# One fused attention and feed-forward kernel on one core: its hand-listed order of steps replaced by another list, with the products of no use gathered in one place

## The chip, the cores and the metric

The kernel runs on one core of a Trainium2 chip. The metric is the time of one execution on the device, in microseconds. A core has a matrix engine (TensorE, "PE" in the profile, with its weight loads as "PEld"), a vector engine (VectorE, DVE), a scalar engine with function tables (ScalarE, ACT), a general engine (GpSimd, POOL) and an engine that here does nothing but issue transfers (SyncE, SP). Each engine takes its own instructions strictly in their listed order and waits, where it must, on the others.

## The reference

```python
# x: (8, 8, 512, 64)   state: (8, 8, 32, 64)   w_in: (512, 2048)   w_out: (2048, 512)
scale = 1 / np.sqrt(64)
a  = softmax(scale * x @ state.T)        # per block and head: 512 x 32
xread = a @ state                        # 512 x 64
a2 = softmax(scale * state @ x.T)        # 32 x 512
sread = a2 @ x                           # 32 x 64
y = concat([xread, sread], rows)         # 8 blocks of 544 tokens, 512 wide (8 heads x 64)
h = y @ w_in                             # 4352 x 2048
g = h * erf(log(1 + exp(h)))
out = g @ w_out                          # 4352 x 512, f32
```

The two weights come in 8-byte floating point, and the kernel turns them into f32 on chip.

## The kernel before

*Stages.* The eight blocks b have 512 tokens each that come from `xread`; the 32 `sread` tokens of all eight blocks are put together into one small unit, the states. The hidden width of 2048 is done in two halves. In half A all blocks go through attention and through the first 1024 hidden columns, with weights held in `w_in` and `wo[0]`; the output rows are stored from SP. Then the second half of both weights is brought back from DRAM (`wi`, `wo`), and half B goes through the same blocks with kept `y` from DRAM; its outputs are added to the stored rows by transfers from POOL, those of the last block by DVE. Most products are computed in two-by-two quarters with seven products in place of eight (names ending in 1 to 7), which needs sums of quarters on DVE (y.1 to y.4, M1 to M4, A1 to A4, T1 to T4).

*Steps and their list.* Every piece of work is a named step, put into a table by `step(name, f, ...)`. The string `ORDER` (from L18) lists all steps by hand; a loop at the kernel's end issues them in that order, and `in_order` ties each instruction to the one before it on its engine, so that the list is the order on PE, DVE, ACT, SP and POOL alike. Nothing else schedules. Waits between engines follow from the tiles that the steps share; a step placed early in the list of an engine makes all behind it on that engine wait for its data.

A word of the form `~k*n` is no step: it is n products of a 128x128 matrix by itself into bank k of PSUM, whose result nothing reads (`warm`, L367). The step `warm` at the very start is eight such products.

*The steps that matter here.* Names with a block number b = 1 to 7 come once for each block.

- The start, block 0. `lx0` to `lx3` load x of block 0 (L282: even ones are issued from ACT, odd ones from SP), `lst0` to `lst8` the states (L287, L306). `x0` to `x3` transpose x on PE (four products each), `x0c` to `x3c` copy the results out of PSUM, `s0` turns block 0's states. `q0`, `q1` are the scores, copied out by `q00c` to `q11c`; `tm0`, `tm1` transpose them; `max`, `less`, `exp`, `sum`, `inv`, `norm` are the softmax of group 0 and 1 on DVE and ACT; `ta0`, `ta1` transpose the weights back.
- The weights. `piece(kind, j)` makes the steps of 256 columns of `w_in` (kind i) or rows of `w_out` (kind o): `i0l0`, `i0l1` load its two halves (L338, 512 KB each, SP), `i0a0` (L342) and `i0a1` (L345) are conversions on ACT, `i0v0`, `i0v1` (L347, L349) on DVE; piece i0 alone is converted in two parts (`i0+a0` ...). `a0` uses another function table of ACT than the softplus and than the error function. Pieces 4 to 7 are kept in DRAM for half B (`i4k` ...).
- Block 0's first unit. `n00`, `n01`, `n02`, `n10`, `n12` multiply the states by `w_in` (L852), `u0`, `u1` transpose the states of the other blocks (L950; they need all of `lst1` to `lst8`), `h0` to `h7` are the hidden columns (L863) with softplus `h0s` ... (through L611) and copies `h0c` ..., `h0e` ... (L878) the error functions of two at a time, `h0g` ... the products with h, `o00` to `o36` the second products (L884), stored by `o0c`, `o0d` ....
- The second attention of block 0: `big`, `wt`, `wz`, `wn` the softmax, `tw0`, `tw1` (transposes on PE) with copies `tw0c`, `tw1c` on ACT into `a2T`, `rd0` (L464) the product of a2 and x, `rn0`, `rt0`, `rc0` what follows it.
- The attention of block b: `a{b}xq0` to `7` load x transposed (L295, SP), `a{b}tx` turn it on DVE, `a{b}s` the scores (L490), the softmax on DVE and ACT down to `a{b}ta`; then the second attention: `a{b}ey` (ACT), `a{b}ty` (DVE, turns), **`a{b}kz` stores the turned weights to DRAM (L529, SP), `a{b}z0` to `z3` load them back in another layout (L300, SP)**, `a{b}x0` to `x3` load x (L290, SP), and **`rd{b}` (L464) multiplies the two on PE**, followed by `rn`, `rt`, `rc`.
- The hidden part of block b: `A{b}m` (L573) multiplies states and `w_in`, `A{b}f01` to `f17` are the products (L622, in `hidden`), with copies (L230) on ACT and softplus (L611) `..s11` to `..s22`, then `e0`, `e1` (error function, L630) and `g0`, `g1` (DVE). `A{b}p10` to `p71` are the second products (L672, in `one_level`), `A{b}d0` to `d3` the stores (L652). `SA`, `SB` are the states' unit in half A and B, `B{b}...` those of half B, whose second products go two levels deep (L738, in `inner`).

*Buffers.* Block b and b+1 share most tiles: `at`, `cv`, the two slots of `ring`, eight PSUM banks. So a step of one block often waits until a step of the block before has read its tile.

Line numbers here and in the profile are those of the kernel before; in the changed kernel every line behind the list has a number one lower.

Of the kernel before, what the change touches and what calls it, by code (L numbers as in the profile page):

```python
# [46 lines left out]
i7a1 a3kz A3f05 y33 a4xq0 A3M4 A3f11 A3f0u2 a3x2 A3f07 a4tx1 A2p11 A3f0s11 y34 A2A1 A3f0u3 i7a0
A3f0c22 A3f04 a3z2 A1pc21 A1pc12 A3f03 a3z1 A3f0c21 i7v0 a3z3 A2p50 A3f1c a4tx3 a3z0 A2pc a3iy
a4xq5 A3f0c12 a4tx0 A3f12 yk2 A2A3 A1d0 A3f16 A3f1c11 yk3 i7v1 A3f0s21 rd3 A1d1 A3f1u2 A3f0s12
A3f17 rn30 A3f0s22 rn31 A2A2 rt3 A3f15 A3f1u3 rc3 a4tx2 A3f14 A3f1c22 a4s A2A4 A3e0 A3f13 a5xq3  # L50
A2p60 A3f1c21 A3f1c12 o4l1 a4c0 A1d3 a4c1 a4tu0 a5xq2 A2p61 a4mx0 a4tu1 yl3 A3f1s11 A1d2 a4my0
A3f1s21 A4m i7k a4mx1 A2pu2 o4l0 A3f1s22 a4my1 a5xq6 A3f1s12 a4sb1 A2p70 a4sb0 a5xq4 a4ex0 a4x3
A2p71 a4ex1 a4sm0 a5xq1 A4m00 a4sm1 A4m01 a4x1 A2p51 A4m10 a4iz o5l1 a4nm0 A2pu3 a5xq5 A4m11 a4ta0
A2p20 a4nm1 a4ms A4M1 A3e1 a4ta1 A4f01 y41 A4M3 A2p40 A4M2 y42 y44 a4ey1 A2p21 a5tx1 A4f0c A3g1
a4ey0 A4f02 A4f06 A4f0c11 A2pc22 A4f05 A4f0u2 a4ty1 A2pc11 y43 A4f11 A4M4 o4a0 A4f07 a4ty0 A3g0
A2p41 a4kz A4f0u3 a5xq7 a4x2 A2p30 A2pc21 A3A3 o4a1 A3A1 A2p31 a4z3 A3p10 A4f0c22 a4z0 a4z1 o4v0
a4x0 a5tx2 A3p11 a5xq0 a5tx3 A3A2 a4z2 A4f04 A2d0 A3pc o4v1 A4f03 A4f0c21 a4iy A3p60 A4f1c A2pc12
o4k yl4 A4f0c12 A2d1 A4f16 A4f0s12 rd4 A4f1u2 A4f0s22 A4f17 A4f0s11 rn41 a5x3 rn40 a5tx0 A4f0s21
A2d3 rt4 A4f15 A3A4 rc4 o5l0 A4f1u3 a5s A4f1c22 A4f14 a5c1 a6xq6 a5c0 A4f13 A4f1c21 a6xq0 a5tu0
A4f12 a5my0 a5x2 A3p20 a5mx0 A4e0 a6xq5 a5tu1 a5sb0 a5x0 A3p61 a5mx1 a6xq4 a5sb1 o6l0 A4f1c12  # L60
A3p50 a5ex0 a6xq3 a5my1 a5ex1 o5a0 a5sm1 a6xq2 A5m a5sm0 a6xq7 a5iz a5ms a5nm0 a5ey0 A3p51 a5nm1
A4f1c11 a5ta0 A5m00 A3pu2 o5v0 A5m11 A5f01 a5ta1 A5m10 y51 A3p70 a5ey1 A5M1 A5m01 y53 y52 A5f0c
a5ty0 A3p71 A5M2 a5ty1 A4f1s22 A5f06 a5iy A5M3 o5a1 a5kz a6xq1 a6tx1 A5f02 A3pu3 A5f05 A5f0u2 o6l1
A3pc22 A5f0c11 a6tx2 A5f07 o5v1 A5f11 A5f0u3 A4f1s21 A3p30 y54 a6tx3 A4f1s11 a5z0 A4f1s12 A4g0
a5x1 a5z2 A5f04 a5z3 A3p31 A4e1 a5z1 a6tx0 A3d3 o5k A5M4 A3p40 yl5 A5f0c22 A2d2 A4g1 A5f0c21 yk4
A5f1c A5f03 o6a1 A5f16 A5f0c12 rd5 A5f1u2 A5f17 rn51 rn50 A4A1 rt5 A5f15 rc5 A5f1u3 a6s A5f1c22
A5f12 A5f0s11 a7xq3 a6c1 A5f14 a6c0 a7xq5 a6tu1 A5f13 A5f1c21 a6my0 A5f0s21 a7xq0 A3p21 A5f1c12
a6tu0 a7xq2 a6mx0 A3p41 A3pc11 a6x1 A4A2 A5f1c11 a7xq4 a6sb0 A4p10 a7xq6 a6mx1 a6ex0 a6my1 A3pc21
a7xq1 A4p11 a6sb1 a6sm0 o7l1 a6ex1 a7xq7 o6a0 a6sm1 A6m a6iz a6x0 A4pc a6nm0 yk5 a6nm1 A4p20 A6m00
a6ms a6ta0 A6m10 A3pc12 A6m11 y61 a6ey0 A6f01 A3d1 a6ta1 a6x3 A6m01 A6M1 A4p60 a6x2 A6f0c a6ty0  # L70
# [6 lines left out]
A7m01 A7m10 a7iz a7nm0 A4p41 a7my0 A4pc11 A7m00 a7ta0 A7m11 A7f01 A7M1 a7nm1 A5p10 A7f0c a7ms y71
a7ey0 a7ta1 a7ey1 A7M2 A7f05 y72 A4pc21 y73 A7f02 A5A3 A4d2 A7f06 A4d1 A6f0s11 a7x1 y74 A5p11 A5A1
o7a1 A4d0 a7x3 a7ty1 A6f1s22 A5p50 A6f0s21 A5A2 A5pc o7a0 a7ty0 A5p60 A7M3 a7kz A6f1s12 A5A4 A5p61
o7v0 o7v1 A5p51 A5pu2 A6f0s12 A6f1s11 A5p70 A7f0u2 A7f0c11 a7z0 A6f0s22 a7z1 A5p71 a7x0 a7z2 a7z3  # L80
A7f07 o7k A5pu3 A6f1s21 A7f11 A5pc22 A7f0u3 a7iy A5d3 A5p30 A7f0s11 yl7 A5p31 A6e1 A7f04 A7f0c22
A7M4 rd7 A7f0c21 A7f1c A7f03 rn71 wo rn70 rt7 A7f16 A7f0c12 A7f12 A7f1u2 A7f15 A7f1c11 rc7 A7f17
# [973 lines left out]
```

## Time and profile before

| | us |
|---|---|
| three runs | 709.36, 711.31, 711.01 |
| their median | 711.01 |
| the profiled execution | 710.65 |
| span of its instructions | 708.9 |
| mean granted clock of PE in it | 0.998 |

The span is what the views below cut up; the profiled execution's own time is 1.75 us longer. The page's slices show where PE is not full: each digit is a fortieth of the span, 17.7 us, in tenths.

```
PE   8879999999999999999999999999999999999997
DVE  4759899978788969566433649698969597889482
ACT  2999998899588866855135675678675675775720
DMA  8867687859677832741051232214333313151535
```

The groups of instructions that PE spends most of its time in, with count, busy time and mean time of one:

| line and step | products | busy us | mean ns |
|---|---|---|---|
| L672, second products of half A | 840 + 168 | 189.8 + 37.7 | 380 |
| L622, hidden products | 480 + 360 | 121.4 + 90.9 | 382, 380 |
| L738, second products of half B (the largest of its groups) | 588 | 73.0 | 275 |

ACT loads a function table 71 times in all, 1.28 us each; of these 31 stand at the softplus (L611), with 39.8 us.

Start of one product to start of the next takes 0.43 us for 128x256, 0.22 for 128x128 at full clock, as the timeline shows them one behind the other.

### The profile page before, as it was taken

How to read it: one execution, taken by the hardware profiler on the slowest of the kernel's cores; microseconds unless marked ns; L12 is line 12 of the kernel's file. 1: busy time of each engine (PE TensorE's matmuls, PEld its weight loads, DVE VectorE, ACT ScalarE, POOL GpSimd, SP SyncE). 2: the span in 40 equal slices, each digit the busy share in tenths (PEclk: the TensorE clock that was granted, in tenths of full speed). 3: DMA queues.
4: the chain of work that ended last, by engine and by line, in shares of the span. 5: the costliest groups of instructions: out<-in, count | busy, mean ns of one | idle time of the engine just before them, and what ended most of it. 6: DMA issues, size and time to landing. Idle time of an engine off the chain costs nothing.

```text
span 708.9 us, 12281 instructions
## 1 busy us (share of the span) xinstructions
PE 695.3 (98%) x4931; PEld 582.1 (82%) x4931; DVE 524.4 (74%) x717; ACT 481.0 (68%) x709; POOL 37.7 (5%) x38
## 2 busy tenths in 40 slices
PE   8879999999999999999999999999999999999997
...
DVE  4759899978788969566433649698969597889482
ACT  2999998899588866855135675678675675775720
...
DMA  8867687859677832741051232214333313151535
GB/s 263 202 190 133 194 200 209 193 179 244 186 172 224 207 130 87 216 147 48 16 193 45 90 111 26 58 21 93 40 73 36 78 19 65 16 97 31 83 75 105
DMA packets 136441, 84.96 MB, mean 120 GB/s; under 512 B 93760, under 2 KB 127552, under 8 KB 136128
## 3 DMA queue, kind: packets, MB, share of 16 engines
...
q10 hardware_dynamic: 544, 0.52, 0.2%
...
## 4 chain that ended last, share of the span: by engine, by line
PE 91%; ACT 4%; DMA 1%; issue 0%; DVE 0%; SPq 0%; DVEq 0%; ACTq 0%
PE b L672 31%; PE b L622 26%; PE b L738 22%; PE b L573 4%; PE b L924 4%; PE b L884 2%; PE b L464 1%; PE b L490 1%; DMA at<-in_x_dram 1%; ACT ring L611 1%; ACT L611 1%; ACT ring L345 0%; ACT L342 0%; ACT ring L230 0%; PE b L863 0%
## 5 line engine op out<-in xcount | busy, mean ns | idle before, releaser
L672 PE MATMUL b<-ta,ring 128*128 128x256 f32 x840 | 189.8, 380 | 0.0
L672 PEld LDWEIGHTS b<-ta,ring 128*128 128x128 f32 x840 | 158.3, 190 | 26.6 <-issue 3.4
L230 ACT COPY ring<-b 128x512 f32<-128x512 f32 (+1 forms) x138 | 79.6, 584 | 86.4 <-PE b L622 63.3
L622 PE MATMUL b<-y,m 128*128 128x256 f32 x480 | 121.4, 382 | 1.4 <-ACT ring L230 1.2
L622 PEld LDWEIGHTS b<-y,m 128*128 128x128 f32 x480 | 88.0, 190 | 17.3 <-issue 3.5
L230 ACT COPY res<-b 128x512 f32<-128x512 f32 (+2 forms) x98 | 52.1, 537 | 71.1 <-PE b L672 35.2
L222 DVE TENSOR_TENSOR ring<-ring,b 128x512 f32<-128x512 f32 (+1 forms) x71 | 46.7, 661 | 67.9 <-PE b L622 25.1
L622 PE MATMUL b<-sy,m 128*128 128x256 f32 x360 | 90.9, 380 | 0.0
L224 DVE TENSOR_TENSOR ring<-ring 128x2048 f32<-128x2048 f32 (+1 forms) x36 | 77.8, 2164 | 9.1 <-ACT ring L630 8.8
L611 ACT ACTIVATE ring<-ring 128x512 f32<-128x512 f32 x128 | 76.4, 629 | 5.3 <-DVE ring L222 5.0
L622 PEld LDWEIGHTS b<-sy,m 128*128 128x128 f32 x360 | 65.7, 190 | 10.2 <-issue 1.3
L223 DVE TENSOR_TENSOR ring<-ring 128x1024 f32<-128x1024 f32 (+2 forms) x65 | 73.2, 1137 | 0.3
L738 PE MATMUL b<-at,ring 128*128 128x128 f32 x588 | 73.0, 275 | 0.0
L738 PEld LDWEIGHTS b<-at,ring 128*128 128x128 f32 x588 | 71.4, 192 | 1.6
L650 POOL DMA_DIRECT2D out_dram<-res x32 | 37.0, 1281 | 664.7 <-DVE res L222 589.4
L222 DVE TENSOR_TENSOR res<-res,b 128x512 f32<-128x512 f32 (+2 forms) x46 | 28.5, 619 | 53.6 <-ACT res L230 27.9
L630 ACT ACTIVATE ring<-ring 128x2048 f32<-128x2048 f32 x30 | 57.4, 1913 | 0.2
L230 ACT COPY b<-b 128x512 f32<-128x512 f32 (+2 forms) x56 | 31.0, 556 | 24.1 <-PE b L672 13.2
L230 DVE STREAM_TRANSPOSE at<-at 128x512 f32<-128x512 f32 x56 | 38.1, 696 | 4.7 <-ACT at L230 4.7
L611 ACT ACT_TABLE_LOAD x31 | 39.8, 1283 | 0.5
L230 ACT COPY m<-b 128x512 f32<-128x512 f32 (+2 forms) x65 | 34.2, 572 | 7.5 <-PE b L573 6.9
L672 PE MATMUL b<-at,ring 128*128 128x256 f32 x168 | 37.7, 380 | 0.0
...
## 6 DMA issues: line engine op xcount, KB each, us to landing
...
```

The costliest lines, as they stand in the source:

```text
L222: add = lambda o, a, b: tt(o, a, b, op=ALU.add)
L223: sub = lambda o, a, b: tt(o, a, b, op=ALU.subtract)
L224: mul = lambda o, a, b: tt(o, a, b, op=ALU.mult)
L230: do[name] = lambda: f(*args)
L573: pe.matmul(out=to[j][k][Ns * p:Ns * p + Ns, :], lhsT=by, rhs=w_in[r, 4 * j:4 * j + 4, i, :], start=True, stop=True)
L611: act.activation(out=o, in_=i, func=ACTF.Softplus)
L622: pe.matmul(out=to[:, i], lhsT=xs[n - 1][:, q:q + P], rhs=ys[n - 1], start=(start and i == 0), stop=(i == 1), skip_group_check=True)
L630: step(u + "e%d" % o, lambda s=s: act.activation(out=s, in_=s, func=ACTF.Erf))
L650: nc.gpsimd.dma_start(out=to, in_=of, accum_op=ALU.add)
L672: pe.matmul(out=to[:, E2 * h:E2 * h + E2], lhsT=a[:, k // 2, k % 2], rhs=rhs[n][:, k], start=(start and h == 0 and k == 0), stop=(k == 3), ...
L738: pe.matmul(out=out_[:, P * j:P * j + P], lhsT=lhs[:, i], rhs=rhs[:, i], start=(start and j == 0 and i == 0), stop=(i == 1), skip_group_ch ...
L924: pe.matmul(out=to[:, P * i:P * i + P], lhsT=xs[n - 1][:, i, k], rhs=ys[n - 1][:, k], start=(start and i == 0 and k == 0), stop=(k == 1), ...
```

## The change

Only the string `ORDER` differs: 144 lines of it became 143. No step is added or taken out; every function is the same. What differs is

1. the order of steps on every engine, from the first line to the last;
2. the words `~k*n`. Before there are six, `~7*7`, `~7*2`, `~7*3`, `~2*16`, `~7*2` and `~6*2`, 32 products, spread between `i0l1` and `n01`; with the step `warm` that makes seven places. After there is one beside `warm`: `~2*17` ahead of `ta0`. PE has 2493 products before and 2478 after.

The start of the list, to the step `A1f01`:

```diff
-warm lst0 lx0 lx1 lx2 lx3 i0l0 i1l1 i1l0 i0l1 ~7*7 s0 i2l0 i2l1 ~7*2 x1 lst3 lst6 x0 x1c lst1 s0c
-lst5 x2 x0c lst7 lst4 q0 lst2 x3 q01c lst8 q00c x2c i3l1 x3c tm0 i3l0 i0a0 q1 i0a1 max0 q10c i0v0
-q11c i0v1 ~7*3 tm1 less0 o0l0 n00 max1 exp0 n00c1 less1 sum0 exp1 i1a0 inv0 sum1 norm0 i1a1 inv1
-i1v0 ~2*16 ta0 i0+a0 norm1 n00c0 ta0c i1v1 ~7*2 ta1 i0+a1 i0+v0 ta1c n02 i0+v1 n02c0 big1 i2a0
-o0l1 ~6*2 n01 h0 big0 a1xq1 n01c0 n01c1 i2a1 big n02c1 a1xq2 y01 h1 i2v0 wt0 a1xq3 i2v1 wt1 u1
-a1xq4 wz wn1 u0 a1xq0 u1c h0s n10 wn0 h0c h2 h1s a1xq5 y02 n10c1 h1c n10c0 o1l0 i3a0 h3 o1l1 a1xq6
-i3a1 i3v0 h4 a1xq7 h2c i3v1 h2s o2l0 h3s o0a1 o2l1 n12 o3l0 h5 n12c1 h3c o3l1 u0c n12c0 h4c tw0
-o0a0 tw1 h4s o0v0 h5s h6 o0v1 tw1c tw0c i4l1 rd0 a1tx2 a1tx0 h0e h7 rn0 h4e h0g h2e rt0 a1tx1 o10
-y04 h5c o1a0 h4g o00 o1a1 o1v0 a1tx3 rc0 o1v1 a1s h7s h2g o20 a1c0 a2xq5 a1c1 a1tu0 h6s a2xq0
-a1tu1 h7c o22 o2a0 a1mx0 i4l0 a1mx1 yl0 h6c o12 a1my0 a2xq2 o2a1 o2v0 a1x2 a1sb0 o02 a1x3 a1sb1
-a2xq1 o2v1 a1ex1 a1ex0 a1x0 A1m a1sm1 o3a0 a2xq4 a1sm0 a1my1 o14 o3v0 h6e a1iz a1nm0 A1m00 o04
-a1nm1 o3a1 a1ms a1ta0 h6g A1m11 A1f01 A1m10 o3v1 o24 y11 a1ey1 A1M1 o06 a1ey0 a1ta1 A1M2 A1f0c
...
+warm lx1 lx0 lst0 lx2 lx3 i0l0 i0l1 i1l0 x1 s0 x0 s0c i1l1 lst2 x2 x0c x1c x3 i3l0 i0a0 x2c q0 x3c
+i0v0 lst3 i0a1 q01c q1 q00c i0+a0 i0v1 tm0 q11c i0+v0 i3l1 q10c i0+a1 n00 lst8 max0 tm1 lst4 n00c1
+less0 i1a0 lst5 max1 i2l1 exp0 less1 i2l0 sum0 exp1 lst1 i1a1 inv0 lst7 sum1 lst6 norm0 i3a0 o0l0
+inv1 i1v0 ~2*17 ta0 i3a1 norm1 a1xq6 i1v1 ta1 n00c0 ta0c i0+v1 ta1c n02 big0 i2a0 o0l1 n01 u1 big1
+a1xq5 n02c0 u0 n02c1 n01c0 i2a1 i2v0 o1l0 h0 a1xq7 big n01c1 u1c wt0 y01 o1l1 i2v1 wt1 a1xq4 h1
+o0a0 a1xq0 i3v0 h0c i3v1 n10 h2 wz o3l0 wn1 h0s o2l0 n10c1 h1s a1xq1 y02 h3 n10c0 a1tx3 h2c a1xq2
+o0v0 h2s h1c a1tx2 n12 o1a1 wn0 h5 o3l1 n12c1 h3c y04 a1xq3 o0a1 tw1 o2l1 h5c o0v1 h4 h3s h5s
+a1tx0 n12c0 i4l0 tw1c tw0 a1tx1 h4s h4c u0c h6 h0e h7 tw0c h0g o1a0 rd0 h4e o1v0 o20 y03 h6c rn0
+yk0 o1v1 h2e a1x0 rt0 o10 o3a1 h4g rc0 h2g o3a0 a1s o2a1 o3v0 o22 a2xq6 o3v1 h7c a1c0 i5l1 a1c1
+a1x3 o00 a1tu0 o2a0 yl0 a1tu1 a1mx0 i4l1 o12 o2v0 a1sb0 a2xq2 h7s o2v1 h6s o02 a1mx1 a1ex0 A1m
+a1sb1 a2xq3 a1sm0 a1ex1 a2xq7 a1my1 a1my0 a1x2 o14 a1sm1 h6e a1iz A1m00 a1nm0 a1x1 o04 A1m11 a2xq4
+a1ta0 A1m10 a1ms i4a1 h6g A1f01 a2xq5 o24 A1M1 a2xq0 a1nm1 a1ey1 y11 a1ta1 o06 a1ey0 A1M2 A1f0c
...
```

Two of the seven places where a block's second attention goes through DRAM, from the store `kz` over the reloads `z` to `rd`; block 2 and block 6:

```diff
-a2ta1 A2M2 A2f0c y21 A2f02 y22 a2ty1 A2f06 A2f0c11 a2ty0 A2f05 A2M3 A2f0u2 a2kz y23 a3xq2 A2f11
-i5v0 A2M4 A2f07 a3xq1 y24 A1p61 i5v1 A2f0u3 a3xq4 A2f0c22 A2f04 a3tx3 A2f0s11 T3 A2f03 a2z2
-A2f0c21 a2z1 A2f0s22 A1p20 A2f0c12 a2x3 A2f1c a2z3 A1A4 A2f0s21 a2z0 i6a1 A2f16 i5k A1A3 o0d A2f12
-A1pu2 yk1 A2f0s12 T4 A1p70 o3d A2f1u2 yl2 a2iy a3tx0 a3tx2 A2f17 A2e0 a3tx1 rd2 A2f15 A2f1u3 rn20
+A2M2 i5a1 y22 a2ty0 A2f06 y23 A2M3 A1p61 A2f0u2 A2M4 a2ty1 a2iy A2f07 a3tx0 a2kz i5v0 A2f05 A2f0u3
+a3tx2 A2f11 y24 A2f0c22 A2f04 A2f0s11 T4 A2f03 A2f0c21 a2z1 A1A4 a2z2 A1p20 A2f1c a2z3 A1pu2 a2z0
+A2f0c12 A2f0s22 i6l0 A2f0s12 i5v1 A2f16 A2f0s21 A2f12 T3 A2f1u2 i7l0 yl2 rd2 yk1 A1A3 A2e0 A2f15
...
-a6ey1 y62 a7tx3 A6f05 a6ty1 A6f02 A6M2 A5f0s12 a6kz A5f0s22 A4A3 A4p61 A3d2 A5f1s21 A5f1s11 a7tx1
-A6f06 y63 A4A4 A4pu2 A4p50 A5f1s12 a6iy A6M3 A6f0c11 A5f1s22 y64 A4p51 o6v0 a7tx0 A6M4 A5e1 A4p70
-a6z3 A6f0u2 A4p71 a6z2 a6z1 a6z0 A6f07 A4pu3 o7l0 A5e0 A3d0 A6f11 A4pc22 yl6 o6v1 A4p30 A6f0u3
-a7tx2 A5g0 A4p31 A6f04 A6f0c22 rd6 A6f0c21 A6f1c A6f03 rn61 a7x2 rn60 A5g1 o6k rt6 A6f16 rc6 yk6
+A6m10 A3p41 a6kz A6m11 a7xq4 A6f0c A6M1 y61 A6f02 A6M2 y63 A5f1s21 A6f05 y62 A3pc11 o5v0 A6f06
+A5f0s12 A4A2 a6z2 A3pc21 a6z1 A4p10 a6z3 a7tx2 a6z0 o6l1 A6M3 a7xq2 A4p11 o5v1 A4A4 o5k rd6 A4pc
```

The rest of the list differs in the same manner, in half B too.

More of the change, by code (lines that the diff above doesn't have):

```diff
@@ L47 @@
[L47 to L70, printed above, removed]
@@ L77 @@
[L77 to L82, printed above, removed]
@@ new lines @@
+A3M4 A3f07 i6v0 A2p10 A3f0u3 A2A1 A3f0c22 a3z1 A3f04 a3z2 a4tx2 a3z3 A3f03 a4tx3 a3z0 A3f0c21
+A1pc12 A2p11 A3f1c A2A2 A3f0c12 A3f16 A3f0s11 i6v1 rd3 A3f1u2 A1pc21 A3f17 rn31 a4x2 rn30 a4tx0
+i6k rt3 A3f15 A2A3 rc3 A3f0s22 a4s A3f1u3 A2A4 A3f14 a4c1 a5xq0 A3f1c22 a4c0 A3f12 a4x1 a4tu0
+a5xq7 A3f13 A3f1c11 a4tu1 A3f1c21 A2p50 a4mx1 A3f1s11 a4my0 a5xq1 A2pc a4mx0 A2p60 A1d1 a4sb1 a4x3
+a4sb0 yl3 a4ex1 A3f1c12 A2p61 a4ex0 a4my1 i7a0 a4x0 a5xq2 a4ms a4sm0 a4ey0 A4m a4sm1 A2pu2 a4iz
+a4nm1 a5xq3 A2p70 a4nm0 A4m11 a5xq5 A4m00 a4ta0 a4ey1 a4ta1 a5xq6 A4f01 A4m10 a4ty1 a5xq4 A4m01
@@ new lines @@
+A2p71 a4ty0 A4f0c A4M1 a4kz y41 A4f02 a4iy A4M2 A3f1s22 A4f05 i7v0 A3f0s21 A3f1s12 A4M3 A2p51
+A2pu3 y42 a5tx2 A4f0c11 a4z0 A3f1s21 y43 a4z2 A4f11 A3f0s12 A2pc22 a4z3 a4z1 i7v1 A4f06 A2d3 yk3
+A2p30 A3e1 a5tx0 o5l0 o4l0 a5tx3 A4M4 rd4 A4f0u2 y44 A3e0 A4f07 rn41 a5x0 rn40 a5tx1 rt4 A2p31
+A3g1 A4f0u3 rc4 A4f04 a5x1 A1d0 A4f0c22 A4f0s11 A2p20 A2pc12 A4f0c21 a5x3 A3g0 A4f1c A4f03 A4f16
+A3A1 a5s A4f1u2 A4f0c12 A4f17 a5c0 a6xq2 a5c1 A4f15 a5tu0 A4f1u3 a6xq1 a5tu1 A4f0s21 A4f12 A4f1c22
+A1d2 A4f14 yl4 a5mx1 a6xq5 A4f13 a5sb1 A4f1c21 a6xq4 a5mx0 A2p21 A4f1c12 a6xq6 a5sb0 a5ex1 A5m
@@ new lines @@
+o7v0 A6p10 yl7 o7v1 A5d1 A7f1c22 A7f14 o7k A6A2 A5d3 A7f13 A7f1c21 A5p41 A7f1s12 A7f1c12 SAV1
+A6p11 A5pc21 SAV3 A5d2 wo A6A3 A6p50 A6pc A7f0s12 A7f0s22 A6p60 A7f1c11 A7f1s21 A6p20 A7e0 A6p61
+A6p21 A7f1s11 TB1 A6pu2 A7f1s22 A6p51 yS2 SAV2 A7g0 A6p70 A6p71 A6A4 TB2 SAf1 A6pu3 A6pc22 A6p40
+A6d3 A7e1 A6p30 A6pc11 A7g1 SAfc A6p41 A7A1 A7p10 A6pc21 A7A3 A6p31 SAV4 A7A2 A7p11 A6pc12 A6d1
+SAf6 yL0 SAf5 SAfu2 A7pc A7p60 SAf7 A7p20 SAfu3 SAfc22 TB3 SAf2 SAfs22 yS4 SAf4 SAfc11 A7p50 wi
+yK0 A6d2 A7p61 SAf3 A7pu2 SAfc21 A7p70 SAfc12 TB4 A7p71 A7A4 SBV1 SBf1 A7pu3 SAfs12 SBV2 A7p51
@@ new lines @@
+SBfc SBV3 SAfs11 A7p21 A7pc22 SBf5 SBf6 t21 SBV4 A7p30 SBfu2 SAfs21 A7p31 SBf7 A7pc12 A7d1 A6d0
+A7p40 t0k SBfu3 SBfc22 t61 SBf4 SAe t62 SBf3 SBfc21 SBf2 SBfc12 SBfs12 SAg SBfs21 B0m SBfc11
+A7pc11 t31 t22 A7p41 SAA1 B0m00 B0m10 B0m01 B0m11 B0f01 SBfs22 B0M1 SAp10 A7pc21 B0M2 B0f0c A7d2
+SAA3 yK1 B0f05 SAA2 A7d3 SApc SBfs11 SAA4 B0f06 B0M3 B0f02 B0M4 SBe SAp60 SAp50 SBg SApu2 SAp70
+B0f0u2 B0f0c11 SBA3 SBA1 B0f11 SApu3 SApc22 B0f07 SAd3 A7d0 SAp30 B0f0u3 t3k B0f04 SApc12 B0f0s11
+B0f0c22 SAd1 SAp40 t01 B0f0c21 B0f1c B0f03 SApc21 B0f16 B0f0c12 t24 SAp20 B0f0s21 SBA2 B0f1u2 t32
@@ new lines @@
+B2f05 B0bc12 B2f04 B2f0c22 B2f11 B1a2 B2f0s22 B2f0c21 B1ap10 B0U2 B2f1c B2f03 B0U3 B2f12 B0U4 B1A4
+B2f16 B1ap11 B2f1u2 B0C2 B1ap50 B1ac B2f0c12 B2f0s12 B0d2 B2f17 B1A3 B2f0s21 B0d3 B1ap60 B2f1c11
+B2f1u3 B1a3 B1ap20 B2f1s11 B2f0s11 B2f15 B1b1 B2f14 B2f1c22 B2e0 B0C12 B1ap61 B1b3 B0d1 B2f13
+B1ap21 B2f1c12 yK4 yK3 B1a4 B1ap51 B1au2 yL3 B1ac11 B1ap70 B1ap71 B2f1s21 B1bp10 B1au3 B2f1c21
+B1ac22 B1bp11 B1ap40 B2f1s12 B1b2 B1ap41 B1ap30 B1ac21 B1bc B1ap31 B2f1s22 B1bp60 B1ac12 B2g0
+B1bp61 B2e1 B1bp20 B1bp50 B1C11 B1bp21 B1bu2 B1bp51 B2g1 B1d0 B1bp70 B1bp71 B3m B1bu3 B1bc22 B1b4
@@ new lines @@
+B4m B2b3 B2bp60 B4m01 B2bp61 B2ap31 B2bu2 B3f1s12 B2bp70 B2ac12 B4m00 B4m10 B2bp71 B3f1s11 B2bp50
+B4m11 B2bp51 B3f1s21 B4M1 B2bp20 B2bu3 B2C11 B2bp21 B4M2 B2d0 B4f01 B2bc22 B3e1 B4M4 B2bp40 B4M3
+B2bp41 B2bp30 B4f0c B3g1 B2bc21 B2bp31 B2bc11 B4f06 B4f02 B4f0u2 B3A1 B3ap10 B4f0c11 B2bc12 B4f07
+B3a1 B4f05 B4f0u3 B2U2 B3ap11 B4f0c22 B4f04 B2U3 B3ac B4f03 B2U4 B4f11 B4f0c12 B4f0s22 B4f0c21
+B2C2 B3ap20 B4f0s21 B4f15 B4f1c B3a2 B2d3 B4f16 B2d2 B2C12 B3ap50 B4f1u2 B3A2 B2d1 B3ap60 B3A3
+B4f17 B3ap21 B3A4 B4f1u3 B4f0s11 B3ap51 B4f0s12 B3b1 B3ap61 B3b3 B4f12 B3a3 B3ac11 B4f14 B3au2
@@ new lines @@
+B3bp10 B4f1c22 yL5 B4f13 B4e0 B3bp11 B4f1c12 yK6 B3ap70 B3b2 B4f1c21 B3ap71 B4g0 B5m B3au3 B3ac22
+B4f1s12 B3ap40 B3a4 B5m11 B3ap41 B5m00 B3ap30 B3ac21 B3bc B3ap31 B4f1c11 B4f1s21 B3bp60 B3ac12
+B5m01 B3bp61 B5f01 B3bu2 B4f1s11 B3bp70 B4f1s22 B5m10 B3bp71 B3bp50 B5M1 B3bu3 B5f0c B3bp51 B5M2
+B3bp20 B3bc22 B3b4 B3bp40 B4e1 B5M3 B3bp21 B5M4 B3bp41 B3bp30 B3bc21 B4g1 B3bc11 B5f06 B3bp31
+B5f0u2 B5f05 B3C11 B5f07 B3bc12 B3d0 B3U2 B5f02 B5f0u3 B4A1 B4ap10 B5f0c11 B5f04 B5f0c22 B3U3
+B5f11 B5f0s22 B4A3 B5f0c21 B4ap11 B5f1c B3U4 B5f03 B4ac B3C2 B5f16 B4ap20 B5f0c12 B5f1u2 B3d3 B4a1
@@ new lines @@
+B5f0s12 B5f15 B3d2 B5f0s21 B5f17 B4A2 B4ap50 B5f1u3 B4a2 B5f0s11 B5f12 B5f1c22 B4ap21 B4A4 B5e0
+B4ap60 B4a3 B5f14 B4ap61 B4b1 yL6 B4ac11 B5f13 B5f1c11 B3C12 B4au2 B4bp10 B5f1c21 B3d1 B5f1c12 yK7
+B4b2 B4bp11 B4ap70 B4b3 B4ap71 B4a4 B4ap51 B4au3 B4b4 B6m B4ac22 B5f1s22 B5f1s21 B4ap40 B6m11
+B5f1s11 B4ap41 B4ap30 B4ac21 B4bc B4ap31 B6m10 B6m01 B4bp60 B4ac12 B6m00 B6M1 B4bp61 B5f1s12
+B4bp50 B4bu2 B6M2 B4bp51 B6M3 B4bp70 B5g0 B5e1 B4bp71 B4bp20 B4bp21 B4bu3 B5g1 B6f01 B4bp40 B6f0c
+B4bp41 B4bc22 B6f06 B6M4 B4bp30 B5A1 B6f0u2 B4bc11 B4bp31 B6f07 B4bc12 B5A2 B6f02 B6f0u3 B4bc21
@@ new lines @@
+B6f05 B5a1 B6f0c11 B6f04 B4C11 B6f11 B6f0c22 B4d0 B4U2 B5ap10 B6f0c21 B4U3 B6f1c B6f03 B4U4 B6f16
+B4C2 B6f0s22 B6f12 B6f1u2 B6f0c12 B5ap11 B4d3 B5a2 B6f17 B5ac B4d2 B6f1c11 B6f15 B5A3 B6f0s11
+B5ap60 B6f0s21 B5A4 B6f1u3 B5ap61 B6f1s11 B5a3 B6f14 B5ap20 B6f1c22 yL7 B4C12 B5ap50 B5a4 B4d1
+B5ap21 B5au2 B6f13 B6f1c21 B6f1s22 B5ap70 B6f0s12 B6f1c12 B5ac11 B5b1 B5ap71 B6f1s12 B6f1s21
+B5bp10 B5b2 B5au3 B5bp11 B5ap51 B5ap40 B6e0 B5ac22 B5ap41 B7m B5ac21 B6g0 B5bc B6e1 B5bp20 B5b3
+B5bp21 B7m00 B5bp60 B6g1 B7m10 B7m11 B5ap30 B5bp61 B5ap31 B7M1 B5bu2 B5bp70 B5ac12 B7M2 B5bp71
```

154 lines of the change are left out of this document (66 added, 88 removed).

## The prediction

> **What bounds the kernel now.** The head of the page comes first: TensorE (PE) is busy for 98% of the span, so time can only come from where PE does nothing, does products of no use, or runs at a lower clock.
>
> ```profile
> span 708.9 us, 12281 instructions
> ...
> PE 695.3 (98%) x4931; PEld 582.1 (82%) x4931; DVE 524.4 (74%) x717; ACT 481.0 (68%) x709; POOL 37.7 (5%) x38
> ```
>
> I then cut the span at two steps that stand at the same place in both lists (below), n10 and A1f01: in this run they start at 27.80 and 66.33 us. Columns: window; its length; busy time and instructions of PE, its weight loads, DVE, ACT, POOL; granted clock; DMA share; GB/s.
>
> ```profile
> 0.00:27.80 27.80, 24.82 (x247) 19.62 (x248) 17.30 (x37) 14.64 (x24) 0.69 (x6) 1.00 0.88 254
> 27.80:66.33 38.53, 33.01 (x210) 14.07 (x210) 25.66 (x41) 37.77 (x50) 0.00 (x0) 0.96 0.75 178
> 66.33:705.00 638.67, 637.45 (x4475) 548.46 (x4475) 480.69 (x639) 428.60 (x638) 37.01 (x32) 1.00 0.44 110
> 705.00:708.90 3.90, 0.00 (x0) 0.00 (x0) 0.75 (x2) 0.00 (x0) 0.00 (x0) 1.00 0.61 156
> ```
>
> After 66.33 PE idles 1.22 us in 638.67: no order can gain more than that there, but a worse one can lose. In the middle window PE lacks 5.5 us and **ACT is the full engine** (37.77 of 38.53). The two neighbouring rows below show the worst place, and PE's waits name what ended it.
>
> ```profile
> 40.80:44.20 3.40, 0.34 (x1) 0.00 (x0) 2.94 (x4) 3.37 (x6) 0.00 (x0) 1.00 1.00 410
> 44.20:47.60 3.40, 2.99 (x66) 2.30 (x67) 1.11 (x3) 3.37 (x4) 0.00 (x0) 0.50 0.59 186
> ```
> ```profile
> PE b L464 <- ACT at L230: 3.5, 1, 3.5
> PE b L852 <- DVE w_in L349: 1.7, 2, 1.1
> PE b L622 <- ACT ring L230: 1.2, 1, 1.2
> ```
>
> PE waits 3.5 us for ACT's copies of a2T (steps tw0c, tw1c) before rd0 (L464), and then has half its clock for 3.4 us. The timeline tells why ACT is late: between 26 and 46 us it loads its function table six times, at 26.52, 30.16, 34.12, 38.76, 41.21 and 44.58, of which the last four are
>
> ```profile
> 34.12 1.28 ACT L611 ACT_TABLE_LOAD   x1
> ...
> 38.76 1.28 ACT L342 ACT_TABLE_LOAD   x1
> ...
> 41.21 1.28 ACT L611 ACT_TABLE_LOAD   x1
> ...
> 44.58 1.28 ACT L878 ACT_TABLE_LOAD   x1
> ```
>
> **The change, part by part.** Work is the same but for 15 products of no use; the order differs everywhere. I count by the three windows.
>
> *Before n10.* PE does the same useful steps in both lists ahead of n10 (x0 to x3, s0, q, tm, n00, ta, n02, n01, u, h0, h1). In the old run s0 started only at 7.10, behind the products of no use, and ta1 at 20.56. In the new list the first transposes (x1) follow the eight opening products (done at 4.33), when a load of x has landed (3.2 to 4.8 us after an issue at 0.74: 4 to 5.5). But x3 (0.87 us, one step of four transposes) now stands before q0, and the clock is low at first, so q0 comes at about 10 to 11, where it came at 10.54: nothing won. The removed products cost nothing and bring nothing here: PE was waiting for the softmax under most of them (the 32 records of "~2*16" end at 19.09, ta0 begins at 19.05 when the normalised weights are there). The opposite pull is on SP: the loads of the states (L306), which stood before the pieces i3, now stand among and behind all eight halves of w_in, the last three at the very end, and u1 needs all eight. Eight halves, x and the states are 5.7 MB; at the 340 to 364 GB/s of the windows from 6.6 to 13.5 us that is some 16 us, from 2.7 us on, so 19 us, and 20.5 to 23.5 with waits for landings (SP's row "SPq L306 <- DMA ring<-in_moe_w_in_dram: 3.7, 2, 2.7" shows such a wait). After u1 and u0 (0.87 each at most) come h0 and h1 (2 x 1.72): n10 at 25.7 to 28.7 by this path, at 27.1 by that of ta1 (21.2, then n02, n01 1.0 and 4.9). I take **28.0**, near the later end of the slower path; bounds 26.5 and 30.8.
>
> *n10 to A1f01.* Again the same set of steps. Useful PE time: 33.01 less half of the 2.99 at clock 0.50, so 31.5. The old losses: 3.5 (rd0), 1.5 (clock), 1.1 (n12 waits for piece i3), 0.44 (h5), 0.3 (tw0): 6.8, and small gaps. In the new list the exponent-building conversions (L342: i3a0, o0a0) come before ACT's first softplus, so up to h0e it loads tables twice (h0s, h0e) where it did six times: 4 x 1.28 = 5.1 us less of the engine that is full. Behind tw0 PE has h6 and h7 (3.4 us) before rd0; behind tw1 also h4 and tw0, in all 1.72 + 0.9 + 3.4 = 6.0 us. ACT's work from tw1c to tw0c is five instructions of 0.6 to 1.1 and one table load, 4.7 us: it fits with about 1 us to spare. i3 is converted (i3v1) five PE steps before n12, h0 to h3 and n10 covering it. What is late next is o20, which needs h0e and then h0g (1.23 us on DVE) and has only rd0 (1.0) in front: 0.6 to 0.8 us of wait. So **32.3**; bounds 31.5 (no wait) and 35 (half of the old loss stays).
>
> *After A1f01.* The table loads are 71 in both; those saved early come back late, when ACT is 68% busy and PE's queue covers them. The part that loses its cover is the **turn through DRAM** of each block's second attention: store kept_z (L529), four reloads (L300), then product rd. PE steps listed between store and rd, at 0.86 us for two of L622, 1.73 for four of L672: old 10.4, 11.2, 9.5, 11.2, 11.2, 15.5, 13.0 us for blocks 1 to 7; new 7.8, 6.9, 7.8, 6.9, 6.9, 6.0, 7.8. What the turn takes when nothing big stands between shows in block 6:
>
> ```profile
> 246.61 0.34 SPq L529 DMA_DIRECT2D kept_z<-at  x1
> ...
> 249.96 1.75 SPq L300 DMA_DIRECT2D at<-kept_z  x4
> ```
>
> The last of four issues starts at 251.3 and lands 3.2 later (median of the row for these transfers): 7.9 us after the store. In the old run rd started 1.2 us later after the store than the listed PE work (mean of seven: 84.0, 118.9, 152.3, 193.6, 225.8, 263.2, 302.4, against stores at 73.1, 106.8, 141.9, 180.3, 213.6, 246.6, 287.6). With that, the new allowances are 9.0, 8.1, 9.0, 8.1, 8.1, 7.2, 9.0: only rd6 misses 7.9, by 0.7, three have 0.2 to spare, and for jitter I add 1.3. The new SP list has at most two small x loads and one more transfer between store and reloads, where the old had x blocks and weights. The old wait of 1.2 at 154.55 (L622) goes. So 637.45 + 2.0 = **639.5**; bounds 638.0 and 645.
>
> *Tail.* The last product and the half stores after it stand as before: 3.9.
>
> Sum: 28.0 + 32.3 + 639.5 + 3.9 = 703.7 against a span of 708.9, 5.2 less. The profiled execution took 710.65, 1.75 more than its span, and the median is 711.01, 0.36 above it: **705.5 us**.
>
> **A rule on the clock.** The rows first: the eight opening products (16 records) take 0.23 us a record, the 32 of "~2*16" 0.12; and after 3.5 us without a product the clock is 0.50 for 3.4 us. The Trainium skill, "TensorE: Matmul & The Clock Gate", Part 1, says that the array is throttled by default and is let go only after a window of some 3.4 us that is busy: taking away the products that filled PE's waits speaks against this change. By that rule the first 10 us or more run at half rate: the second rival. The trace agrees as far as the window at 44.2 goes; whether the new start stays busy enough no run here shows yet.
>
> **Rivals.**
> *The turn through DRAM sets the pace (slower).* In six of seven old blocks store to last landing took 8.3 to 11.0 us. Should the new spans be 10.0, the waits are 1.0, 1.9, 1.0, 1.9, 1.9, 2.8, 1.0: 11.5 instead of 2.0, so 705.5 + 9.5 = 715. It decides from 9.4 on. For it: SP takes its list in order, and one late issue moves all behind it. Against: those old spans had x blocks or weights between.
> *A cold start.* Steps x1 to q0 at half rate take 9.4 us from 4.4, 1.0 later than q1's old start; tm and n00 another 1.0; the 17 products need 3.4 us at half and 2.1 at full rate, 5.5 against 4.8 that the softmax takes from tm1 to ta0: 0.7. In all 2.7: 708.2. For it the 0.23 us records; against, loads land before 5.5, so PE is idle for 1 us only.
> *The middle gains nothing.* ACT stays full there and something else of it (h0e before tw0c) holds rd0 as long: 6 us back, 711.
>
> **How the numbers follow.** Forecast 0.5 (own range 702 to 708.5), cold start 0.2, turn 0.2, nothing gained 0.1. This kernel's measurement tells 0.3%, 2.1 us, from no change. Faster by more: nearly all of the forecast, half of the cold start, 0.6; within: 0.17, from the cold start and the last case; slower: the turn and a little, 0.23. Range 700.5 to 713.5: all bounds at their best give 701.7; above, part of the turn's case is left out.
>
> **What would show it.** Right: two table loads on ACT from 26 us to h0e; rd0 (first L464) with under 1 us of wait and no 0.50 row after it; A1f01 near 60.3; PE idle some 2 us after it, in front of L464. Wrong: a clock of 0.50 or 0.2 us records past 8 us; L852 or L950 waiting past 24 us; L464 waiting 1 us or more in most blocks; new waits of PE in the second half, where I expect none.

## The result and the profile after

| | before | changed |
|---|---|---|
| median of four runs, us | 710.86 | 706.42 |
| lowest to highest | 709.36 to 711.31 | 705.04 to 707.63 |
| profiled execution, its span | 710.65, 708.9 | 707.63, 705.7 |

The ratio is 0.9941 with a 95% interval of 0.9917 to 0.9965: faster, by 0.35% to 0.83%. The changed kernel's profiled execution is the longest of its four; the spans of the other three are 704.4, 702.6 and 704.1.

The windows of the changed kernel, cut at the same two steps as before: n10 now starts at 30.81 and A1f01 at 62.70, and the last product ends at 701.85. Columns as in the prediction's windows (length; PE, its weight loads, DVE, ACT, POOL; granted clock; DMA share; GB/s).

```profile
0.00:30.81 30.81, 24.46 (x217) 17.12 (x217) 19.72 (x39) 18.28 (x28) 0.69 (x6) 0.83 0.99 275
30.81:62.70 31.89, 31.68 (x210) 13.73 (x210) 25.11 (x39) 30.39 (x44) 0.00 (x0) 1.00 0.80 208
62.70:701.85 639.15, 637.95 (x4476) 548.45 (x4474) 480.64 (x638) 431.69 (x639) 37.06 (x32) 1.00 0.44 109
701.85:705.70 3.85, 0.00 (x0) 0.00 (x0) 0.75 (x2) 0.00 (x0) 0.00 (x0) 0.93 0.31 104
```

So the start took 3.0 us more (27.80 to 30.81), the middle 6.6 less (38.53 to 31.89), the rest took 0.5 more (638.65 to 639.15, to the last product's end), the tail is as it was. In the middle ACT's busy time fell from 37.77 to 30.39 at the same PE work. The timeline says why; these are all of ACT's table loads between 20 and 48 us, where there were six:

```profile
29.53 1.28 ACT L610 ACT_TABLE_LOAD   x1
...
40.98 1.28 ACT L877 ACT_TABLE_LOAD   x1
```

In both kernels every load of this stretch stands in front of a softplus or behind one. The table of the error function serves the conversion `a0` too, other than the list of steps has it: in the changed kernel one stands at 43.70 between two error functions (L877), without a load.

PE's waits in the changed kernel, longest first (engine, line, what released it; us in total, times, longest):

```profile
PE b L404 <- DVE ring L223: 2.4, 2, 1.5
PE b L949 <- DMA at<-in_x_dram: 1.4, 1, 1.4
PE b L851 <- ACT m L229: 1.1, 1, 1.1
PE b L463 <- DMA at<-kept_z: 0.9, 2, 0.5
```

Of the 3.5 at rd0 only 0.2 are left, and the 1.1 at n12 are gone. The first three new ones all lie in the start: ta0 and ta1 wait for the softmax (L404), n02 for a copy (L851), u1 for the last state load (L949). The profile puts the wait of u1 down to a load of x; the one that landed just before u1 began, at 23.45 against 23.76, is lst6, the last of the states. What these waits set off stands in the windows of the start:

```profile
13.60:17.00 3.40, 2.10 (x19) 1.91 (x18) 2.36 (x6) 2.74 (x4) 0.00 (x0) 1.00 1.16 285
17.00:20.40 3.40, 1.49 (x8) 0.86 (x8) 3.37 (x8) 2.12 (x3) 0.00 (x0) 0.80 1.16 317
20.40:23.80 3.40, 1.67 (x33) 0.76 (x34) 1.81 (x4) 2.57 (x7) 0.00 (x0) 0.50 1.09 269
23.80:27.20 3.40, 3.40 (x10) 2.37 (x11) 3.29 (x7) 3.00 (x8) 0.00 (x0) 0.50 0.99 274
27.20:30.60 3.40, 3.40 (x6) 1.18 (x5) 2.06 (x5) 2.45 (x3) 0.00 (x0) 0.69 0.94 237
```

PE is busy for about half of 13.6 to 23.8, the granted clock falls to 0.50, and the first big products behind u1 run at that: h0 takes 3.41 us and h1 2.12, where 1.72 is their time at full clock. In the kernel before the clock is 1.00 in all of these windows.

### The profile page after: what moved, and what is told of

Read it like the earlier page. It is cut to its first block, busy times and chain, and to the rows that moved or that the text cites. A ratio compares the mean times of both kernels' runs of the same rounds, so it can differ in the third digit from the quotient of the medians.

```text
span 705.7 us, 12193 instructions
## 1 busy us (share of the span) xinstructions
PE 694.1 (98%) x4901; PEld 579.3 (82%) x4901; DVE 526.2 (75%) x717; ACT 480.4 (68%) x709; POOL 37.8 (5%) x38
## 4 chain that ended last, share of the span: by engine, by line
PE 86%; DMA 6%; ACT 3%; SPq 3%; DVE 1%; issue 1%; DVEq 0%; ACTq 0%
PE b L671 27%; PE b L621 24%; PE b L737 22%; PE b L923 3%; PE b L572 3%; PE b L883 3%; PE b L862 2%; SPq L294 1%; DMA st<-in_state_dram 1%; DMA w_in<-kept_in 1%; DMA at<-in_x_dram 1%; PE b L463 1%; DMA at<-kept_z 1%; PE b L489 1%; DMA kept_z<-at 1%
## 5 line engine op out<-in xcount | busy, mean ns | idle before, releaser
L671 PE MATMUL b<-ta,ring 128*128 128x256 f32 x840 | 191.9, 380 | 0.1
L737 PE MATMUL b<-at,ring 128*128 128x128 f32 x588 | 74.8, 275 | 0.0
L229 ACT COPY b<-b 128x512 f32<-128x512 f32 (+2 forms) x56 | 30.8, 554 | 26.9 <-PE b L671 15.9
```

What stands on the lines that cost most here:

```text
L229: do[name] = lambda: f(*args)
L671: pe.matmul(out=to[:, E2 * h:E2 * h + E2], lhsT=a[:, k // 2, k % 2], rhs=rhs[n][:, k], start=(start and h == 0 and k == 0), stop=(k == 3), ...
L737: pe.matmul(out=out_[:, P * j:P * j + P], lhsT=lhs[:, i], rhs=rhs[:, i], start=(start and j == 0 and i == 0), stop=(i == 1), skip_group_ch ...
```

## The experiments

Eleven kernels; each is one of the two lists with an edit, every function unchanged but for one (tables). n10, A1f01 and "the rest" (from A1f01 to the last product's end) are read from the one profiled execution of each, the time is the median of 5 to 12 runs, the ratio is to the kernel before on the same chip (711.1 to 711.5 for the eleven, which ran on three chips).

| | n10 | middle | A1f01 | rest | us | ratio, 95% interval |
|---|---|---|---|---|---|---|
| before | 27.80 | 38.53 | 66.33 | 638.65 | 710.86 | |
| changed | 30.81 | 31.89 | 62.70 | 639.15 | 706.42 | 0.9917 to 0.9965 |
| e4_new_start | 30.30 | 32.15 | 62.45 | 638.63 | 706.71 | 0.9928 to 0.9952 |
| e8_tables | 30.31 | 38.28 | 68.59 | 639.20 | 712.22 | 1.0010 to 1.0030 |
| e1_fill | 27.93 | 32.46 | 60.39 | 639.62 | 705.63 | 0.9913 to 0.9936 |
| e2_states_early | 28.50 | 33.91 | 62.41 | 638.24 | 706.18 | 0.9918 to 0.9952 |
| e10_no_fill | 29.37 | 32.46 | 61.83 | 638.17 | 706.11 | 0.9916 to 0.9943 |
| e7_old_no_fill | 26.21 | 38.20 | 64.41 | 638.61 | 708.99 | 0.9954 to 0.9980 |
| e11_one_place | 25.25 | 38.90 | 64.15 | 638.64 | 708.27 | 0.9946 to 0.9971 |
| e3_old_start | 27.32 | 39.74 | 67.06 | 638.98 | 712.27 | 1.0011 to 1.0030 |
| e5_old_rest | 29.74 | 31.87 | 61.61 | 638.60 | 705.84 | 0.9919 to 0.9942 |
| e6_rd_later | 29.10 | 32.28 | 61.38 | 642.63 | 709.83 | 0.9971 to 0.9988 |
| e9_fill_old_rest | 27.80 | 32.03 | 59.83 | 638.86 | 704.86 | 0.9898 to 0.9926 |

### What made the middle shorter: table loads, or PE's order?

e4_new_start: the changed list to n10, then the old order of what is left.

```diff
 (the changed list up to i3v1)
-n10 h2 wz o3l0 wn1 h0s ... tw1 ... h4 h3s h5s ... tw0 ... h6 h0e h7 tw0c ... rd0
+... wz wn1 h0s n10 ... h3 h4 h2c h2s ... n12 ... h5 ... tw0 tw1 h4s ... h5s h6 o0v1 tw1c tw0c i4l1 rd0
```

> The changed list up to n10, and from there the steps not yet listed in the old list's order. The conversions i3a0 and o0a0 then stand ahead of the first softplus, as in the changed list, but PE has tw0, tw1 and h6 alone ahead of rd0, as in the old one. Theory (ACT's table loads held up the middle): two table loads from 26 us to h0e, the wait at rd0 under 1.5 us where the old one was 3.5, A1f01 at 63.5 to 65, 708 us. Rival (what stands on PE between tw and rd0 made the difference): rd0 waits 3 us or more and half clock follows, A1f01 near 68, 713 us.

The middle is 32.15 long, 0.3 more than in the changed kernel, with PE's old order between tw and rd0; A1f01 comes at 62.45, earlier even than the theory's 63.5. No wait at rd0 is left among PE's waits. The rival falls: PE's order there is worth next to nothing. What e4 shares with the changed kernel is the whole list up to n10, and with it that i3a0 and o0a0 stand ahead of h0s. Whether it is these two, and not the earlier loads and conversions, e8 tells.

e8_tables: the other way round, the changed list with the table loads put back.

```diff
+        step("xt%d" % k, lambda k=k: act.activation(out=extra[:, k:k + 1], in_=ident[:, k:k + 1],
+                                                    func=ACTF.Prelu, alpha=-2.0 ** 32))
...
-o0v0 h2s h1c ... h4 h3s h5s
+o0v0 xt0 h2s h1c ... h4 h3s xt1 h5s
```

> The changed list with two added ACT operations on a single column, of the function that the weight conversions use, one ahead of h2s and one ahead of h5s: they put back four table loads (two there, two back) where the old list had them, and nothing else moves. Theory (table loads): ACT has four more loads of 1.28 and two short operations, 5.4 us in all, up to tw0c; ACT had no time to spare there (the wait at rd0 was 0.2), so rd0 comes 4 to 5.4 later, PE idles for over 3 us and may lose its clock; A1f01 at 66.5 to 68, 711 us. Rival (the new PE order covers them with h6 and h7, or with what follows): rd0 waits under 2, 707.5 us.

In its timeline ACT's loads up to h0e are

```profile
29.29 1.28 ACT L610 ACT_TABLE_LOAD   x1
33.52 1.28 ACT L947 ACT_TABLE_LOAD   x1
35.02 1.28 ACT L610 ACT_TABLE_LOAD   x1
40.89 1.28 ACT L947 ACT_TABLE_LOAD   x1
42.39 1.28 ACT L610 ACT_TABLE_LOAD   x1
46.03 1.28 ACT L877 ACT_TABLE_LOAD   x1
```

six as in the old kernel, and a loss of the old size is back at the same time:

```profile
40.80:44.20 3.40, 0.30 (x1) 0.00 (x0) 2.16 (x4) 3.37 (x6) 0.00 (x0) 1.00 0.60 186
44.20:47.60 3.40, 3.00 (x8) 1.64 (x9) 0.00 (x0) 3.37 (x7) 0.00 (x0) 0.70 0.05 17
```

PE stands still for 3 us and has a lower clock after it. The place is another: PE waits 3.5 in front of tw0 (L404), for a copy that stands on ACT behind the second added operation, where the old kernel waited in front of rd0; a wait of 1.8 at a hidden product (L862), for a softplus behind the first one, comes on top. The middle is 38.28 long, 6.4 more than without the two short operations, and the whole gain is gone (712.22). Two operations on a single column cost 5.8 us together, because each brings two table loads to the engine that is full. From load to load (33.52 to 35.02) a switch with its operation takes 1.50. The Trainium skill, "ScalarE: Activation LUTs", section "What ACT_TABLE_LOAD costs", counts 2.66 us for every switch, the 1.28 of the load and a drain of 1.38; for four switches that gives an estimate of 10.6. The trace has the 1.28 and no such drain: the next operation starts at 34.81, 0.01 after the load's end.

### What made the start longer: the loads, or the clock?

e1_fill: more products of no use in the changed list, where PE waited.

```diff
-~2*17 ta0 ... ta1 ... n02 ... n01 u1
+~2*23 ta0 ... ~3*4 ta1 ... ~3*5 n02 ... n01 ~3*7 u1
```

> The changed list with 22 more products of no use where PE waited in its trace: ~2*23 for ~2*17 ahead of ta0, and ~3*4, ~3*5, ~3*7 ahead of ta1, n02 and u1. Theory (the start loses to the clock): the granted clock stays 1.00 from 17 to 31 us, where it was 0.50 for about 10, u1 still starts at 23.8 (the last state load lands at 23.45), h0 and h1 take 1.72 each where they took 3.41 and 2.12, n10 at 27.8 to 28.3 where it was 30.8; 703.7 us (-2.7). Rival (the loads alone set the start): n10 stays at 30.5 or later, since the products only fill waits; 706.4.

The clock is 1.00 in every window, and n10 is at 27.93, 2.9 earlier, with u1 at 23.61 where it was 23.76: the theory holds for n10. Of it 2.3 are left at A1f01. In the time 2.7 was expected and only 0.8 is seen, and the runs of the two overlap (705.04 to 706.26 against 705.04 to 707.63): no gain in time is shown. Part of that lies in the comparison: the changed kernel's profiled execution was its slowest, and the same start came out at 30.30, 29.74, 29.10 and 30.31 for n10 in the profiles of e4, e5, e6 and e8. And rd3 now waits 1.4 for its reload of kept_z.

e2_states_early: the last state loads earlier.

```diff
-lst5 max1 i2l1 exp0 less1 i2l0 sum0 exp1 lst1 i1a1 inv0 lst7 sum1 lst6
+lst5 max1 lst1 lst7 lst6 i2l1 exp0 less1 i2l0 sum0 exp1 i1a1 inv0 sum1
```

> The changed list with the state loads lst1, lst7, lst6 ahead of both halves of i2 on SP. Theory (u1 waits for the last state load): the states have landed near 20.5, u1 starts behind n01 at 22.0 to 22.3 instead of 23.76, n10 about 1.5 earlier at 29.3, as the clock stays low; 704.9 us. Rival (the clock alone matters): n10 within 0.4 of 30.8; 706.4. i2 is converted about 0.8 later, and n10 waits for it if that is too late: then n10 at 30.0 to 31.5.

u1 starts at 22.47, 1.3 earlier, and n10 at 28.50: the loads count too. That is 2.3 earlier than in the changed kernel's profile, but only 0.6 earlier than the earliest of the five executions of the unchanged start (29.10). A1f01 gains only 0.3, and the time (706.18) is not the 704.9 expected. Two of PE's waits in this kernel:

```profile
PE b L404 <- DVE ring L223: 2.3, 2, 1.5
PE b L883 <- DVE ring L223: 1.5, 1, 1.5
```

The second is new: o20 waits for h0g on DVE, which stands behind a transpose of x (a1tx1) whose data have just landed. PE got ahead of the loads of x and gave part of the gain back.

e10_no_fill: the changed list without its one group of products of no use, ~2*17.

> The changed list without its ~2*17. Theory (these 17 end 1.5 us before ta0 and save nothing that the following waits don't lose anyway): ta0 at 17.2, the clock is 0.50 from 15 or 16 us instead of 19.5, back at full by 27 to 29, n10 at 30 to 31, 706.4 us within 1. Rival (the 17 products hold the clock for tm1, ta0 and the transposes): n10 at 32 or later, 707.5 us or more.

By its windows (0.89 from 13.6 to 17.0, 0.50 to 20.4, 0.60 from 23.8 to 27.2) the clock goes down near 16.3 us and is back near 26.5, in the changed kernel near 19.1 and 29.3: the stretch at half clock is as long and lies earlier. n10 is at 29.37 and the time 706.11, no different from the changed kernel. The 17 products are worth nothing there.

### Products of no use in the old list

e7_old_no_fill takes all six groups out of the old list; e11_one_place takes them out and puts ~2*17 where ~2*16 stood, which is this part of the change done alone.

```diff
-i0l0 i1l1 i1l0 i0l1 ~7*7 s0 i2l0 i2l1 ~7*2 x1 ... ~7*3 tm1 ... ~2*16 ta0 ... ~7*2 ta1 ... ~6*2 n01
+i0l0 i1l1 i1l0 i0l1 s0 i2l0 i2l1 x1 ... tm1 ... ~2*17 ta0 ... ta1 ... n01
```

> The old list without its 32 products of no use behind the step warm. Theory (they hold the clock up): the clock falls to 0.50 somewhere between 5 and 25 us, h0 and h1 take up to 3.4 each, n10 at 30.5 to 32 where it was 27.8, 713.5 us or more. Rival (PE would have waited there anyhow and the clock plays no part): n10 at 27.5 to 28, 711 us.

> The old list with this part of the change alone: its six groups of products of no use taken out, ~2*17 put where ~2*16 stood. Theory (the old products ahead of s0 and x1 were in the way, and those ahead of ta0 keep the clock): s0 at 4.5, q1 near 10.3, n10 at 25.5 to 26.2, the clock 1.00 up to n10; with the middle and the rest as in the old run 2 us less, 708.8 us. Rival (part of the gain of this list without any such product came from leaving out those ahead of ta0): n10 at 27 or later, 710.5 us or more.

Both are faster than the kernel before, e7 by 0.20% to 0.46% and e11 by 0.29% to 0.54%. The expectation for e7 failed in its main point: the clock does fall (0.50 from 17.0 to 20.4 us), and yet n10 comes 1.6 earlier; the rival's n10 at 27.5 to 28 and 711 us were missed too. The timeline of the old kernel shows what was in the way,

```profile
4.33 2.84 PE L367 MATMUL b<-ident 128*128 128x128 f32 x14
7.10 0.66 PE L392 MATMUL b<-ident,ring 128*64 128x128 f32 x8
```

and that of e11 what follows without it:

```profile
4.46 0.93 PE L392 MATMUL b<-ident,ring 128*64 128x128 f32 x8
5.77 1.53 PE L385 MATMUL b<-ident,at 128*128 128x128 f32 x12 [0.38 <-DMA at<-in_x_dram]
```

Seven products of no use (~7*7) kept s0 (L392) until 7.10 though its data had landed; without them it starts at 4.46, and the whole chain of block 0's softmax with it. In e11 ta0 comes at 16.74 instead of 19.05 and n10 at 25.25 instead of 27.80, with the granted clock at 1.00 up to there.

e3_old_start: the old list to h0s, then the changed order of what is left.

> The old list up to h0s (the step before n10), its products of no use with it, and from there the steps not yet listed in the changed list's order; i3a0, i3a1 and o0a0 then come at once, ahead of h0s. Theory (the two gains and the one loss stand apart): n10 at 27.8 as in the old run, two table loads up to h0e, the middle 31.9 to 32.5 long, A1f01 at 59.7 to 60.3, the rest 639.2; 704.6 us. Rival (ACT and the loads of x are late behind the old start): the middle takes 34 or more, A1f01 at 62 or later, 706.6 us or more.

The theory's sum did not come, the rival did, and stronger than it said: n10 is early (27.32), but the middle takes 39.74, with only two table loads up to h0e. One line of DVE's and one of ACT's timeline (start; duration; in brackets the idle time before and what ended it):

```profile
37.68 0.71 DVE L230 STREAM_TRANSPOSE at<-at 128x512 f32<-128x512 f32 x1 [7.40 <-DMA at<-in_x_dram]
```
```profile
39.96 1.15 ACT L345 ACTIVATE cv<-cv 128x1024 uint32<-128x1024 uint32 x1 [6.20 <-DMA cv<-in_moe_w_out_dram]
```

The changed order turns x on DVE (a1tx3) ahead of n12's copy and converts o1 on ACT early, since its own SP order has loaded both early; behind the old start these loads are issued late, both engines stop for 6 to 7 us, and PE waits 4.3 for the copy. So the joint does not show what an early start with few table loads is worth. It shows that the order of the loads on SP and the order on DVE and ACT belong together.

### The rest

e5_old_rest: the changed list to A1f01, then the old order.

> The changed list up to A1f01, and from there the old list's order. Theory (all of the gain stands ahead of A1f01, the rest is worth nothing): A1f01 at 62.7, from there to the end 642.6 as in the old run, where the changed one took 643.0; 706.0 us, with no waits for the reloads of kept_z. Rival (the rest has a share in the gain): 707.5 or more. Rival (the turns through DRAM cost the changed list 2 us or more): 704.4 or less.

The rest takes 638.60, as before, and the time is 705.84: no share of the gain stands behind A1f01. A cost of the changed order there is not shown either. Its rest took 638.17 to 639.62 in the six profiles that have it unedited (the 639.15 among them), the old one 638.60 to 638.86 in six.

e6_rd_later: three of the products behind the turn through DRAM one PE step later (A3f17, A4f07, A4p60); the other words between are steps of other engines.

```diff
-rd3 A3f1u2 A1pc21 A3f17 rn31
+A3f1u2 A1pc21 A3f17 rd3 rn31
...
-rd4 A4f0u2 y44 A3e0 A4f07 rn41
+A4f0u2 y44 A3e0 A4f07 rd4 rn41
...
-rd6 A4pc o7l1 A5f1s12 a7xq7 A4p60
+A4pc o7l1 A5f1s12 a7xq7 A4p60 rd6
```

> The changed list with rd3, rd4 and rd6 two PE steps later each (behind A3f17, A4f07 and A4p60). Theory (these three miss the reload of kept_z): PE's waits of 0.1, 0.7 and 0.5 there go, no new ones come, 0.9 to 1.2 less behind A1f01 (638.0 where it was 639.15), 705.4 us. Rival (what follows rd is as late): the same waits appear at rt or at the next block's scores, 706.4 us.

The waits for kept_z go, and 3.5 us more come in the rest than before the edit. Three of PE's waits:

```profile
PE b L473 <- DVE sn L471: 2.1, 3, 0.9
...
PE b L621 <- ACT ring L229: 1.5, 2, 0.8
...
PE b L671 <- ACT b L229: 0.7, 1, 0.7
```

rd stood between a product and ACT's copy of the bank that the next product needs (A3f16, A3f1u2, A3f17), and covered that copy; and the steps behind it covered DVE's work between rd and rt. The 0.9 us that the changed list waits there (the row of L463 above) is less than what the place is good for.

### The best of them

e9_fill_old_rest joins e1 and e5.

> Both edits that measured as gains together: the changed list up to A1f01 with the 22 more products of no use, and from A1f01 the old list's order. Theory (they add): A1f01 at 60.4 as with the products alone, 638.6 behind it as with the old rest alone, no waits for kept_z; 704.6 us. Rival (one of the two was the spread of runs): 705.5 or more.

704.86, with A1f01 at 59.83 and the rest 638.86: the best median of all, 1.6 below the changed kernel's, though the runs of the two overlap (704.33 to 707.14 against 705.04 to 707.63), and so do the intervals of their ratios; that it is faster than the changed kernel is not shown. Against the kernel before it is 0.74% to 1.02% faster.

## Why the prediction was right, and where it was off

By its terms, against the profiled execution:

| | forecast | bounds | measured |
|---|---|---|---|
| n10 | 28.0 | 26.5 to 30.8 | 30.81 |
| n10 to A1f01 | 32.3 | 31.5 to 35 | 31.89 |
| after A1f01 | 639.5 | 638.0 to 645 | 639.15 |
| tail | 3.9 | | 3.85 |

*The middle* was right in mechanism and size: two table loads where there were six, 0.2 of wait at rd0, no window at half clock behind it. e4 and e8 show that it is the table loads; the other half of the argument, that PE's new order gives tw0c more cover, is not borne out (e4 has the old order and 32.15). The forecast had tw0c fit with 1 us to spare, and rd0 waited 0.2 for it. The 0.6 to 0.8 us named for o20 as late next did not come: it starts 1.03 after rd0, right behind it. In e2, where PE gets there earlier, it waits 1.5.

*The turn through DRAM* was sized well: rd3, rd4 and rd6 came 0.1, 0.6 and 0.4 late, 1.1 in all, where 2.0 were counted (they started 0.44, 0.88 and 0.74 after the product record before them; where rd does not wait, it is 0.31). Store to last landing takes 7.9, 7.5, 7.6, 7.5, 8.1, 8.0 and 6.9 us for blocks 1 to 7, where 7.9 was taken; in block 6

```profile
233.20 0.34 SPq L528 DMA_DIRECT2D kept_z<-at  x1
233.59 1.38 SPq L294 DMA_DIRECT2D at<-in_x_dram  x2
236.08 1.73 SPq L299 DMA_DIRECT2D at<-kept_z  x4
```

the last reload lands at 241.2 and rd6 starts at 241.36. The rival (10.0 and 715 us) needed 9.4 and did not come: the SP list between store and reloads is as short as counted.

*The start* is the step that failed, in two places; with 30.81 it lies at the very end of its bounds, 0.01 beyond. "The removed products cost nothing and bring nothing here" was wrong: that PE waits under the last group says nothing of the first, which held s0 back by 2.6 us. Taken out of the old list alone (e11), this part is worth 2.5 us at n10 and 0.3% to 0.5% of the time. In the changed kernel too q0 starts at 7.6, where 10 to 11 was taken, and ta0 at 17.20 instead of 19.05. There this does not show at n10, since another chain ends last there: the loads of the states, of which the prediction said that u1 could start at 20.5 to 23.5. It started at 23.76. Second, the products behind u1 were priced at full clock. The rival of the cold start had the mechanism and the wrong place: x1 to q1 kept their pace, but between 15.7 and 23.8, where PE waits for softmax and states, the clock went down, and h0 and h1 cost 2.1 us more than 1.72 each. e1 shows the size: n10 at 27.93 with the clock held, against the 28.0 of the forecast. That the two fit so well is partly chance, since u1 came later than the forecast's path had it.

The start was 2.8 longer and the middle and the rest 0.75 shorter than taken: 2.0 above the forecast of 705.5, and the profiled execution took 2.1 more. It is the longest of four, and the median lies 1.2 below it; so 0.9 of the error in the start is left in the result. The forecast's own terms give 705.8 for the median (703.7, 1.75 and 0.36); 705.5 leaves out the last. That the result lies so near is in part luck: the terms that were taken too long offset a quarter of the start's error, and the median run was faster than the profiled one.

What stays open: how early n10 could come with both the changed middle and the removed products' gain (e11's 25.25). e3 was to tell and stumbled over its loads. e9 has ACT busy for 31.90 of the 32.03 us of its middle, so an earlier start alone would meet a full engine; that was not tried.
